# Moving the q and k transposes of a fused attention and gated-MLP kernel from TensorE to the DMA crossbar

## Chip, cores and metric

One core of one Trainium2 chip. The metric is the device time of one execution in microseconds (us); lower is better. Every quoted time is a median of several runs on one chip, unless it is said to be a single run. A verdict (faster, same, slower) compares a kernel with the kernel before by runs of the same rounds on the same chip, in the fast state only; some executions fall into a slower state, with a lower granted clock (the share of its full speed that the chip grants TensorE) and a time some per cent longer.

## The reference, cut to what matters

```python
# q, k, v: (8 batches, 8 heads, 576 tokens, 64); w_phi: (64, 128)
def phi(x):
    proj = einsum('bhsd,df->bhsf', x, w_phi)
    proj = proj - max(abs(proj), axis=-1)
    return concatenate([exp(proj), exp(-proj)], axis=-1)
q_p, k_p = phi(q), phi(k)
kv  = einsum('bhsf,bhsd->bhfd', k_p, v);  z = sum(k_p, axis=2)
num = einsum('bhsf,bhfd->bhsd', q_p, kv); den = einsum('bhsf,bhf->bhs', q_p, z) + 1e-6
x   = num / den                       # heads joined: (8, 576, 512)
h   = relu(x @ w_in);  u, v = halves(h)
out = (u * (w_spatial @ layernorm(v) + b_spatial)) @ w_out
```

Both projections of `phi` contract over the 64 features of a head, and both kernels feed TensorE q and k with features on the partitions (the 128 rows of on-chip memory). They arrive with tokens there. Something has to transpose them, and that is what the change is about.

## The kernel before

The work of the first half (attention features) is cut into 36 units: 32 "pairs" (two heads of one batch, 512 tokens) and 4 "shared tails" (the last 64 tokens of two batches, all heads). Unit 0 is the tail of the first two batches, units 1 to 4 are batch 0, 5 to 8 batch 1, 9 the next tail, 10 to 13 batch 2, and so on. The changed kernel swaps the first two: there unit 0 is the first pair of batch 0 and unit 1 the tail. The second half (gated MLP) is a queue of tasks, dealt out between the units at `RATE` tasks a unit.

```python
def load(b, parts=1):                                # landing tiles: two buffers each
    d = dict(q=ld.tile([P, H, NB * D], BF16, tag="q_bf"), k=ld.tile([P, H, NB * D], BF16, tag="k_bf"),
             v=ld.tile([P, H * NB, D], FP32, tag="v_f"))
    ...                                              # k and q by GpSimd (f32 to bf16 on the way)
    nc.sync.dma_start(out=d["v"]..., in_=main_ap(v, b))                  # v by SyncE

def a_transpose(u):                                  # one unit ahead of its use
    pt = psum.tile([P, 2, 4, P], BF16, tag="bank")
    for i, x in enumerate((src["k"], src["q"])):
        for j in range(4):
            nc.tensor.transpose(out=pt[:, i, j, :], in_=blk, identity=ident)     # L191
    nc.scalar.copy(out=u["kT"], in_=pt[:, 0])                                    # L194
    nc.vector.tensor_copy(out=u["qT"], in_=pt[:, 1])                             # L195

def a_keys(u):      # projection of k on TensorE, max on VectorE, exp on ScalarE
def a_scale(u):     # em = exp(-max) on ScalarE; vs = v * em on GpSimd (two multiplies, about 1.04 us each)
def a_kv(u):        # TensorE: kf^T vs, needs vs
...
for i in range(NU + 4):
    step(i)
    if i == 0:
        load(1); load_weights()                      # w_in, w_spatial, w_out by GpSimd
    elif u and u["pair"] and u["pj"] == 0 and 1 <= u["b"] < B - 1:
        b = u["b"] + 1
        load(b)                                      # one batch ahead
        if b % 2 == 0: load_tail(b // 2)
```

GpSimd therefore does two things in one order: it issues all k, q and weight loads, and it multiplies v. That order is not the order of this source text: when the kernel is built, a scheduler sorts the instructions of each engine.

Of the kernel before, what the change touches and what calls it, by code (L numbers as in the profile page):

```python
# [16 lines left out]
def kernel(  # L17
# [54 lines left out]
    def load_tail(g):  # L72
        d = dict(
            q=ld.tile([P, H, D], BF16, tag="q_tl", name="q_tl", bufs=2),
            k=ld.tile([P, H, D], BF16, tag="k_tl", name="k_tl", bufs=2),
            v=ld.tile([P, H, D], FP32, tag="v_tl", name="v_tl", bufs=2),
        )
        gs[g] = d
        for t, x in ((d["k"], k), (d["q"], q)):
            for i in range(2):  # L80
                nc.gpsimd.dma_start(out=t[i * TL:(i + 1) * TL], in_=tail_ap(x, 2 * g + i))
        for i in range(2):
            nc.sync.dma_start(out=d["v"][i * TL:(i + 1) * TL], in_=tail_ap(v, 2 * g + i))

    def load(b, parts=1):
        d = dict(
            q=ld.tile([P, H, NB * D], BF16, tag="q_bf", name="q_bf"),
            k=ld.tile([P, H, NB * D], BF16, tag="k_bf", name="k_bf"),
            v=ld.tile([P, H * NB, D], FP32, tag="v_f", name="v_f"),
        )  # L90
        st[b] = d
        n = H // parts
        for i in range(parts):
            nc.gpsimd.dma_start(out=d["k"][:, i * n:(i + 1) * n], in_=main_ap(k, b, i * n, n))
            nc.gpsimd.dma_start(out=d["q"][:, i * n:(i + 1) * n], in_=main_ap(q, b, i * n, n))
        nc.sync.dma_start(out=d["v"].rearrange("p (h c) d -> p h (c d)", h=H), in_=main_ap(v, b))
# [7 lines left out]
    make_identity(nc, ident)  # L104
    load_tail(0)
    load(0, parts=4)
# [75 lines left out]
    def a_transpose(u):  # L182
        src = st[u["b"]] if u["pair"] else gs[u["g"]]
        pt = psum.tile([P, 2, 4, P], BF16, tag="bank", name="pt")
        for i, x in enumerate((src["k"], src["q"])):
            for j in range(4):
                if u["pair"]:
                    blk = x[:, 2 * u["pj"] + j // 2, (j % 2) * P:(j % 2 + 1) * P]
                else:
                    blk = x[:, 2 * j:2 * j + 2, :]  # L190
                nc.tensor.transpose(out=pt[:, i, j, :], in_=blk, identity=ident)  # L191
        u["kT"] = a1.tile([P, 4, P], BF16, tag="kT", name="kT")
        u["qT"] = a1.tile([P, 4, P], BF16, tag="qT", name="qT", bufs=3)
        nc.scalar.copy(out=u["kT"], in_=pt[:, 0])  # L194
        nc.vector.tensor_copy(out=u["qT"], in_=pt[:, 1])  # L195
# [28 lines left out]
    def a_scale(u):  # L224
        em = small.tile([P, 2, H], FP32, tag="em", name="em")
        for s, sc in ((0, -1.0), (1, 1.0)):
            nc.scalar.activation(out=em[:, s, :], in_=u["mk"], func=AF.Exp, bias=0.0, scale=sc)  # L227
        if u["pair"]:
            pj = u["pj"]
            vs = feat.tile([P, 2, H, DS], BF16, tag="vs", name="vs", bufs=4)  # L230
            for s in range(2):
                nc.gpsimd.tensor_tensor(out=vs[:, s, :, 0:D], in0=st[u["b"]]["v"][:, pj * H:(pj + 1) * H, :],  # L232
                                        in1=em[:, s, :].unsqueeze(2).to_broadcast([P, H, D]), op=ALU.mult)
            nc.gpsimd.tensor_copy(out=vs[:, :, :, D:DA].rearrange("p i n o -> p i (n o)"), in_=em)
            u["vs"] = vs
        else:
            d = gs[u["g"]]
            vs = vst[u["g"] % 2]
            for bl in range(2):
                r = slice(bl * TL, (bl + 1) * TL)  # L240
                for s in range(2):
                    nc.gpsimd.tensor_tensor(out=vs[r, bl, s, :, 0:D], in0=d["v"][r],
                                            in1=em[r, s, :].unsqueeze(2).to_broadcast([TL, H, D]), op=ALU.mult)
                nc.gpsimd.tensor_copy(out=vs[r, bl, :, :, D:DA].rearrange("p i n o -> p i (n o)"), in_=em[r])
# [224 lines left out]
    for g in range(G):  # L469
        units.append(dict(pair=False, g=g, i=len(units)))  # L470
        for b in (2 * g, 2 * g + 1):
            for pj in range(NP):
                units.append(dict(pair=True, g=g, b=b, pj=pj, i=len(units)))
    NU = len(units)
# [29 lines left out]
    RATE = 4.0  # L504
# [8 lines left out]
    def step(i):  # L513
        n, u, w, z, y, x = (unit(i + d) for d in (1, 0, -1, -2, -3, -4))
        if i == 0:
            a_transpose(u)
        if u:
            a_keys(u)
            a_scale(u)
# [7 lines left out]
        if n:  # L527
# [76 lines left out]
```

## Time and profile before

| | before |
|---|---|
| time, median of 3 (range) | 343.94 us (343.77 to 346.18) |
| profiled span, granted clock | 346.0 us, 0.985 |
| busy TensorE / VectorE / ScalarE / GpSimd | 292.3 / 269.5 / 235.1 / 139.2 us |
| start of unit 1 / 9 / 19 / 35 | 20.8 / 70.5 / 151.4 / 284.7 us |

### The profile page before, as it was taken

The numbers are of one execution on the slowest core, as the hardware profiler recorded it, in microseconds if no ns is written. First come the engines' busy times: TensorE is split into PE (matmuls) and PEld (weight loads), VectorE is DVE, ScalarE is ACT, GpSimd is POOL, SyncE is SP. The second block draws the span as 40 slices with busy tenths as digits, with TensorE's granted clock in tenths as the row PEclk, the third lists the DMA queues.
The fourth block names the chain that finished last, engine by engine and source line by source line (L and its number), as shares of the span: only waits on it lengthen the run. The fifth ranks groups of instructions, "written<-read, shape, count | busy, mean of one in ns | idle before, by whom it ended". The sixth has DMA issues, their size and how long they took to land.

```text
span 346.0 us, 8470 instructions
## 1 busy us (share of the span) xinstructions
PE 292.3 (84%) x3370; PEld 196.6 (57%) x3370; DVE 269.5 (78%) x696; ACT 235.1 (68%) x514; POOL 139.2 (40%) x199
## 2 busy tenths in 40 slices
PE   0266888877899799998888999997986999999995
PEld 0155766545566567665655766765654766655441
DVE  5397999696795999979988997878788798375350
ACT  3089887757659687798867856985975845642723
POOL 8479936654243344264543342524234222001010
PEclk9998999998999999999999999999998999999999
DMA  7999994921029402930374019630000000520404
GB/s 179 221 184 196 194 206 56 140 81 31 2 24 237 122 2 25 240 118 2 34 92 121 3 10 156 247 109 2 3 1 2 2 0 16 200 63 0 140 0 136
DMA packets 45372, 31.13 MB, mean 90 GB/s; under 512 B 14546, under 2 KB 40210, under 8 KB 45332
## 3 DMA queue, kind: packets, MB, share of 16 engines
q0 software_dynamic: 27536, 11.71, 27.7%
q1 hardware_dynamic: 17796, 18.88, 17.9%
q8 instruction: 26, 0.43, 0.5%
q14 instruction: 14, 0.11, 0.1%
HBM read 32.85 MB, written 9.44 MB: 122 GB/s over the span
## 4 chain that ended last, share of the span: by engine, by line
DVE 41%; PE 35%; ACT 8%; POOL 7%; DMA 4%; issue 2%; POOLq 0%; SPq 0%; ACTq 0%
PE po L451 9%; DVE mk L212 7%; DVE mq L221 6%; DVE stats L362 4%; PE ps L428 4%; ACT kf L215 4%; PE pu L407 4%; DVE x L306 4%; PE ps L200 3%; DVE uT L431 3%; PE pq L270 3%; DMA q_tl<-in_q_dram 3%; DVE mhl L250 3%; DVE mhl L251 3%; DVE vn L387 2%; POOL rstd L369 2%
## 5 line engine op out<-in xcount | busy, mean ns | idle before, releaser
L232 POOL TENSOR_TENSOR vs<-v_f,em 128x512 bf16<-128x512 f32 x64 | 65.5, 1043 | 93.5 <-ACT em L227 88.2
L215 ACT ACTIVATE kf<-ps 128x512 bf16<-128x512 f32 x144 | 76.3, 623 | 25.5 <-DVE mk L212 24.9
L283 ACT ACTIVATE qf<-pq 128x512 bf16<-128x512 f32 x128 | 66.6, 622 | 26.7 <-PE pq L270 26.2
L212 DVE TENSOR_REDUCE mk<-ps 128x4 f32<-128x512 f32 x72 | 46.8, 676 | 2.2 <-PE ps L200 2.0
L221 DVE TENSOR_REDUCE mq<-ps 128x4 f32<-128x512 f32 x72 | 46.0, 676 | 0.0
L407 PE MATMUL pu<-xT,w_in_bf 128*128 128x512 bf16 x128 | 34.3, 393 | 3.8 <-DVE x L306 1.2
L453 ACT COPY ob<-po 128x512 f32<-128x512 f32 (+1 forms) x38 | 22.9, 606 | 20.8 <-issue 12.5
L266 PE MATMUL pq<-qT,wphi 128*128 128x256 bf16 x128 | 31.7, 274 | 4.3 <-DVE kv L300 2.1
L362 DVE BATCH_NORM_STATS2 stats<-vr 128x6 f32<-128x512 bf16 (+1 forms) x38 | 25.5, 676 | 12.2 <-ACT vr L361 12.0
L359 PE MATMUL pv<-w_in_bf,xT 128*128 128x512 bf16 x128 | 32.2, 379 | 3.0 <-DVE mq L221 1.7
L428 PE MATMUL ps<-w_spT,vn 128*128 128x512 bf16 x128 | 34.0, 380 | 0.7 <-DVE vn L387 0.7
L270 PE MATMUL pq<-mT,sel 128*128 128x128 bf16 x256 | 28.0, 222 | 5.5 <-DVE mT L256 5.5
L451 PE MATMUL po<-w_out_bf,uT 128*128 128x512 bf16 x128 | 31.8, 379 | 0.1
L194 ACT COPY kT<-pt 128x512 bf16<-128x512 bf16 x36 | 22.2, 617 | 13.9 <-PE pt L191 11.8
L200 PE MATMUL ps<-wphi,kT 128*128 128x256 bf16 x144 | 23.6, 280 | 7.0 <-ACT kT L194 3.2
L270 PEld LDWEIGHTS <-sel 128*128 128x128 bf16 x256 | 22.9, 99 | 11.5 <-issue 9.2
L361 ACT ACTIVATE vr<-pv 128x512 bf16<-128x512 f32 (+1 forms) x38 | 23.1, 624 | 8.6 <-PE pv L359 8.2
L296 PEld LDWEIGHTS <-kf 128*128 128x128 bf16 x512 | 23.8, 99 | 6.9 <-issue 1.3
L431 DVE TENSOR_TENSOR uT<-ps,uT 128x512 bf16<-128x512 f32 x32 | 21.8, 683 | 7.5 <-PE ps L429 7.5
L315 PEld LDWEIGHTS <-qf 128*128 128x128 bf16 x512 | 20.4, 97 | 11.0 <-issue 6.3
L409 ACT ACTIVATE uT<-pu 128x512 bf16<-128x512 f32 x32 | 19.6, 618 | 9.3 <-PE pu L407 9.1
L306 DVE TENSOR_TENSOR x<-pn,rc 128x256 bf16<-128x256 f32 x64 | 25.4, 416 | 0.5
(108 smaller groups left out, 606.4 us busy)
## 6 DMA issues: line engine op xcount, KB each, us to landing
v_f<-in_v_dram SPq DMA_DIRECT2D x8, 1024.0 KB, 8.5
out_dram<-ob SPq DMA_DIRECT2D x32, 256.0 KB, 2.5
k_bf<-in_k_dram POOLq DMA_DIRECT2D x7, 512.0 KB, 6.2
q_bf<-in_q_dram POOLq DMA_DIRECT2D x7, 512.0 KB, 7.9
v_tl<-in_v_dram SPq DMA_DIRECT2D x8, 128.0 KB, 4.5
w_in_bf<-in_moe_w_in_dram POOLq DMA_DIRECT2D x1, 1024.0 KB, 8.7
out_dram<-ob SPq DMA_DIRECT2D x8, 128.0 KB, 2.3
k_tl<-in_k_dram POOLq DMA_DIRECT2D x8, 64.0 KB, 8.0
```

The source lines that it names most:

```text
L200: nc.tensor.matmul(out=ps[:, 2 * x:2 * x + 2, :], lhsT=xT[:, 2 * half + x, :], rhs=wphi2, start=True, stop=True)
L212: nc.vector.tensor_reduce(out=u["mk"][:, hs], in_=pk, axis=AX.X, op=ALU.max, apply_absolute_value=True)
L215: nc.scalar.activation(out=u["kf"][:, s, hs, :], in_=pk, func=AF.Exp, bias=0.0, scale=sc)
L221: nc.vector.tensor_reduce(out=u["mq"][:, 4 * half:4 * half + 4], in_=pq, axis=AX.X, op=ALU.max, apply_absolute_value=True)
L232: nc.gpsimd.tensor_tensor(out=vs[:, s, :, 0:D], in0=st[u["b"]]["v"][:, pj * H:(pj + 1) * H, :], in1=em[:, s, :].unsqueeze(2).to_broadcast( ...
L270: nc.tensor.matmul(out=pq[:, 2 * par + x, :], lhsT=sel[:, j, :], rhs=m, start=False, stop=(x == 1))
L283: nc.scalar.activation(out=qf[:, s], in_=pq, func=AF.Exp, bias=0.0, scale=sc)
L306: nc.vector.tensor_tensor(out=x, in0=pn[r, :, 0:D], in1=rc[r].to_broadcast([n, 4, D]), op=ALU.mult)
L362: nc.vector.bn_stats(out=stats[r], in_=dst[r])
L407: nc.tensor.matmul(out=pu, lhsT=w_in_bf[:, kc, dc * P:(dc + 1) * P], rhs=d["xT"][:, kc, :], start=(kc == 0), stop=(kc == KC - 1))
L428: nc.tensor.matmul(out=ps, lhsT=d["vn"][:, sp, cs], rhs=w_spT[:, sp, 0:T0], start=(sp == 0), stop=False)
L451: nc.tensor.matmul(out=po[r], lhsT=lhs(dc), rhs=w_out_bf[:, dc, :], start=(dc == 0), stop=(dc == KC - 1))
```

## The change

Its intent: let the DMA crossbar do the transposes, so that TensorE loses 288 of them and ScalarE and VectorE lose 36 PSUM copies each. The diff, cut to its core:

```diff
+    def load_heads(b, h0, n):
+        for x, t in (("k", k), ("q", q)):
+            src = d[x][:, h0:h0 + n]
+            nc.gpsimd.dma_start(out=src, in_=main_ap(t, b, h0, n))
+            nc.sync.dma_start_transpose(out=d[x + "T"][:, 2 * h0:2 * (h0 + n), :],
+                                        in_=src.rearrange("p h x -> p (h x)"))
     (tile declarations)
-            q=ld.tile([P, H, NB * D], BF16, tag="q_bf", name="q_bf"),
-            k=ld.tile([P, H, NB * D], BF16, tag="k_bf", name="k_bf"),
+            q=ld.tile([P, H, NB * D], BF16, tag="q_bf", name="q_bf", bufs=1),
+            k=ld.tile([P, H, NB * D], BF16, tag="k_bf", name="k_bf", bufs=1),
+            kT=ld.tile([P, 2 * H, P], BF16, tag="kT", name="kT"),
+            qT=ld.tile([P, 2 * H, P], BF16, tag="qT", name="qT"),
     (tails: the same, k_tl, q_tl and v_tl from two buffers to one)
-    load_tail(0)
-    load(0, parts=4)
+    alloc(0); load_heads(0, 0, 4); load_tail(0); load_v(0); load_heads(0, 4, 4)
-    def a_transpose(u): ...                          # the 8 transposes and 2 copies
+    def a_transposed(u): ...                         # only picks slices of kT, qT
+        eng = nc.vector if u["i"] < 2 else nc.gpsimd # v scaling of the first two units
+    units[0], units[1] = units[1], units[0]          # batch 0 ahead of the first tail
-    RATE = 4.0
+    RATE = 4.1
```

More of the change, by code (lines that the diff above doesn't have):

```diff
@@ L73, in load_tail @@
         d = dict(
-            q=ld.tile([P, H, D], BF16, tag="q_tl", name="q_tl", bufs=2),
-            k=ld.tile([P, H, D], BF16, tag="k_tl", name="k_tl", bufs=2),
-            v=ld.tile([P, H, D], FP32, tag="v_tl", name="v_tl", bufs=2),
+            q=ld.tile([P, H, D], BF16, tag="q_tl", name="q_tl", bufs=1),
+            k=ld.tile([P, H, D], BF16, tag="k_tl", name="k_tl", bufs=1),
+            v=ld.tile([P, H, D], FP32, tag="v_tl", name="v_tl", bufs=1),
+            kT=ld.tile([P, NP, P], BF16, tag="kT_t", name="kT_t", bufs=2),
@@ L77, in load_tail @@
+            qT=ld.tile([P, NP, P], BF16, tag="qT_t", name="qT_t", bufs=2),
         )
         gs[g] = d
-        for t, x in ((d["k"], k), (d["q"], q)):
+        for t, x in (("k", k), ("q", q)):
             for i in range(2):
-                nc.gpsimd.dma_start(out=t[i * TL:(i + 1) * TL], in_=tail_ap(x, 2 * g + i))
+                nc.gpsimd.dma_start(out=d[t][i * TL:(i + 1) * TL], in_=tail_ap(x, 2 * g + i))
+            nc.sync.dma_start_transpose(out=d[t + "T"], in_=d[t].rearrange("p h d -> p (h d)"))
@@ L82, in load_tail @@
         for i in range(2):
             nc.sync.dma_start(out=d["v"][i * TL:(i + 1) * TL], in_=tail_ap(v, 2 * g + i))
-    def load(b, parts=1):
-        d = dict(
-            q=ld.tile([P, H, NB * D], BF16, tag="q_bf", name="q_bf"),
-            k=ld.tile([P, H, NB * D], BF16, tag="k_bf", name="k_bf"),
+    def load_heads(b, h0, n):
+        d = st[b]
+        for x, t in (("k", k), ("q", q)):
[3 more added lines that the diff above has]
+                                        in_=src.rearrange("p h x -> p (h x)"))
@@ L89, in load, with load_v, alloc @@
+    def load_v(b):
+        nc.sync.dma_start(out=st[b]["v"].rearrange("p (h c) d -> p h (c d)", h=H), in_=main_ap(v, b))
+    def alloc(b):
+        st[b] = dict(
+            q=ld.tile([P, H, NB * D], BF16, tag="q_bf", name="q_bf", bufs=1),
+            k=ld.tile([P, H, NB * D], BF16, tag="k_bf", name="k_bf", bufs=1),
+            kT=ld.tile([P, 2 * H, P], BF16, tag="kT", name="kT"),
+            qT=ld.tile([P, 2 * H, P], BF16, tag="qT", name="qT"),
             v=ld.tile([P, H * NB, D], FP32, tag="v_f", name="v_f"),
@@ L90, in load @@
         )
-        st[b] = d
-        n = H // parts
-        for i in range(parts):
-            nc.gpsimd.dma_start(out=d["k"][:, i * n:(i + 1) * n], in_=main_ap(k, b, i * n, n))
-            nc.gpsimd.dma_start(out=d["q"][:, i * n:(i + 1) * n], in_=main_ap(q, b, i * n, n))
-        nc.sync.dma_start(out=d["v"].rearrange("p (h c) d -> p h (c d)", h=H), in_=main_ap(v, b))
+    def load(b):
+        alloc(b)
+        load_heads(b, 0, H)
+        load_v(b)
     wphi2 = cpool.tile([P, 2 * F], BF16)
@@ L104 @@
     make_identity(nc, ident)
+    alloc(0)
+    load_heads(0, 0, 4)
     load_tail(0)
-    load(0, parts=4)
+    load_v(0)
+    load_heads(0, 4, 4)
     w_in_bf = cpool.tile([P, KC, DFF], BF16)
@@ L179, in transpose_spatial, with a_transposed @@
             nc.vector.tensor_copy(out=w_spT[row:row + 1, NB + bl, T0:S], in_=bsp_row[row:row + 1, T0:S])
-    def a_transpose(u):
-        src = st[u["b"]] if u["pair"] else gs[u["g"]]
-        pt = psum.tile([P, 2, 4, P], BF16, tag="bank", name="pt")
-        for i, x in enumerate((src["k"], src["q"])):
-            for j in range(4):
-                if u["pair"]:
-                    blk = x[:, 2 * u["pj"] + j // 2, (j % 2) * P:(j % 2 + 1) * P]
-                else:
-                    blk = x[:, 2 * j:2 * j + 2, :]
-                nc.tensor.transpose(out=pt[:, i, j, :], in_=blk, identity=ident)
-        u["kT"] = a1.tile([P, 4, P], BF16, tag="kT", name="kT")
-        u["qT"] = a1.tile([P, 4, P], BF16, tag="qT", name="qT", bufs=3)
-        nc.scalar.copy(out=u["kT"], in_=pt[:, 0])
-        nc.vector.tensor_copy(out=u["qT"], in_=pt[:, 1])
+    def a_transposed(u):
+        if u["pair"]:
+            js = slice(4 * u["pj"], 4 * u["pj"] + 4)
+            u["kT"], u["qT"] = st[u["b"]]["kT"][:, js, :], st[u["b"]]["qT"][:, js, :]
+        else:
+            u["kT"], u["qT"] = gs[u["g"]]["kT"], gs[u["g"]]["qT"]
     def by_token(xT, half):
@@ L231, in a_scale @@
             for s in range(2):
-                nc.gpsimd.tensor_tensor(out=vs[:, s, :, 0:D], in0=st[u["b"]]["v"][:, pj * H:(pj + 1) * H, :],
+                eng.tensor_tensor(out=vs[:, s, :, 0:D], in0=st[u["b"]]["v"][:, pj * H:(pj + 1) * H, :],
                                         in1=em[:, s, :].unsqueeze(2).to_broadcast([P, H, D]), op=ALU.mult)
-            nc.gpsimd.tensor_copy(out=vs[:, :, :, D:DA].rearrange("p i n o -> p i (n o)"), in_=em)
+            eng.tensor_copy(out=vs[:, :, :, D:DA].rearrange("p i n o -> p i (n o)"), in_=em)
             u["vs"] = vs
@@ L241, in a_scale @@
                 for s in range(2):
-                    nc.gpsimd.tensor_tensor(out=vs[r, bl, s, :, 0:D], in0=d["v"][r],
+                    eng.tensor_tensor(out=vs[r, bl, s, :, 0:D], in0=d["v"][r],
                                             in1=em[r, s, :].unsqueeze(2).to_broadcast([TL, H, D]), op=ALU.mult)
-                nc.gpsimd.tensor_copy(out=vs[r, bl, :, :, D:DA].rearrange("p i n o -> p i (n o)"), in_=em[r])
+                eng.tensor_copy(out=vs[r, bl, :, :, D:DA].rearrange("p i n o -> p i (n o)"), in_=em[r])
             d["vs"] = vs
@@ L473 @@
                 units.append(dict(pair=True, g=g, b=b, pj=pj, i=len(units)))
+    units[0], units[1] = units[1], units[0]
+    units[0]["i"], units[1]["i"] = 0, 1
     NU = len(units)
@@ L513, in step @@
     def step(i):
-        n, u, w, z, y, x = (unit(i + d) for d in (1, 0, -1, -2, -3, -4))
-        if i == 0:
-            a_transpose(u)
+        u, w, z, y, x = (unit(i - d) for d in range(5))
         if u:
+            a_transposed(u)
             a_keys(u)
@@ L526, in step @@
         fill(0.25)
-        if n:
-            a_transpose(n)
         if w:
```

## The prediction

> **What bounds the kernel now.** I read the shares by engine first, then the 40 slices, then the chain that ended last, then the groups that the change touches, then sums over one steady stretch.
>
> ```profile
> PE 292.3 (84%) x3370; PEld 196.6 (57%) x3370; DVE 269.5 (78%) x696; ACT 235.1 (68%) x514; POOL 139.2 (40%) x199
> ...
> PE   0266888877899799998888999997986999999995
> DVE  5397999696795999979988997878788798375350
> ...
> DMA  7999994921029402930374019630000000520404
> ```
>
> No engine is at its limit for the whole span. TensorE and VectorE trade the lead, ScalarE follows. TensorE has next to nothing in the first two slices (17 us), and at the right end (from about slice 33) it is near 9 while VectorE falls to 3 to 7. The DMA row is full for six slices and mostly idle afterwards.
>
> ```profile
> DVE 41%; PE 35%; ACT 8%; POOL 7%; DMA 4%; issue 2%; POOLq 0%; SPq 0%; ACTq 0%
> ```
>
> So the chain that sets the end hops between VectorE and TensorE, and the transfers have 4% of it. Followed in order of time, that is one transfer at the start and one of 4.86 us near 111 us:
>
> ```profile
> 4.97 9.84 DMA q_tl<-in_q_dram
> 14.81 0.14 issue
> 14.95 0.60 PE pt L191 x4
> 15.54 0.02 issue
> 15.56 0.59 ACT kT L194
> 16.16 0.05 issue
> 16.20 0.62 PE ps L200 x2
> ```
>
> The columns are start, length, what. The shared tail of the first two batches is loaded first, nothing real starts before its last piece has landed, and the first projection runs at 16.20 us.
>
> The groups that go (count, then busy us and mean ns, then idle before):
>
> ```profile
> L194 ACT COPY kT<-pt 128x512 bf16<-128x512 bf16 x36 | 22.2, 617 | 13.9 <-PE pt L191 11.8 <-PE pt L255 1.9
> L195 DVE COPY qT<-pt 128x512 bf16<-128x512 bf16 x36 | 14.9, 414 | 10.3 <-ACT kT L194 10.3
> L191 PE MATMUL pt<-ident,k_bf 128*128 128x128 bf16 x128 | 12.9, 225 | 0.2 <-DVE x L306 0.2
> L191 PE MATMUL pt<-ident,q_bf 128*128 128x128 bf16 x128 | 12.7, 222 | 0.0
> ```
>
> Third, a steady stretch from 100 us to the last unit's transposes, and the final part:
>
> ```profile
> 100.00:283.00 183.00, 165.95 (x1987) 114.39 (x1985) 156.46 (x403) 141.23 (x316) 72.03 (x99) 0.99 0.34 73
> 283.00:346.00 63.00, 57.85 (x530) 31.22 (x526) 33.91 (x90) 28.82 (x54) 6.36 (x11) 1.00 0.23 76
> ```
>
> The columns after the length are busy us of TensorE, its weight loads, VectorE, ScalarE, GpSimd, then the granted clock, DMA share and GB/s. In 183 us, TensorE is busy 91%, VectorE 85%, ScalarE 77%. The stretch holds 23 of the 36 units (23 copies of L195), so a unit takes 7.96 us. After 283 us only the second half of the kernel is left, 92% TensorE, and the change takes nothing from it.
>
> **What the Trainium skill says.** "VectorE: DVE Perf Modes", section "The three transpose paths", gives 390 ns for a 128x128 bf16 transpose on TensorE and 1309 ns through the DMA crossbar. The trace has 222 to 225 ns for one on TensorE, and eight in a row hold the chain for 0.45 us, so here they are pipelined and cheaper than the page's figure. The crossbar figure can't be checked in the kernel before, which has none. "DMA: Bandwidth & Descriptors", section "Latency and other measured facts", gives 261 GB/s for DMA transposes in one case and 350 to 400 when contiguous; its "Silent corruption: two transposing streams in flight at once" says that source rows of 256 bytes are what is moved. Its "Rules for kernel authors" asks a DMA that reads what an earlier one wrote to wait on that one's completion semaphore. The built kernel does so: each transpose on the SyncE queue waits for its GpSimd load. The page's two figures differ widely in what they mean here, and this is the main uncertainty.
>
> **The change part by part.**
>
> *Removed.* 288 transposes on TensorE (36 units x 8): 0.45 us a unit where they lie on the chain, 16.2 us in all; by busy time 13.49 us in the steady stretch, 0.59 us a unit. 36 copies on ScalarE, 22.2 us, 0.62 a unit. 36 copies on VectorE, 14.9 us, 0.41 a unit. One PSUM bank in a unit, which two engines had to empty. What of it lies on the chain now: I added its pieces over the whole span and got 19 pieces of L195 (6.3 us), ten groups of L191 (4.65 us) and five of L194 (2.6 us), 13.6 us. The rest ran beside other work.
>
> *What it is worth in the steady part.* Two ways. If a unit shrinks by what leaves VectorE, 0.41 us; if TensorE's 91% stays and its work falls from 165.95 to 152.46 us, the stretch takes 152.46/0.907 = 168 us, 15 us less, or 0.65 a unit. The chain sum is (13.6 - 1.2 for the first unit)/35 = 0.35 a unit, but that keeps every other wait: the pieces "copy of kT, then projection" in which one engine waits for another go altogether, and 13.9 and 10.3 us of idle time stand before those copies. I take 0.5 us for 33 units: 16.5 us.
>
> *Added.* 26 crossbar transposes on the SyncE queue, of 288 blocks of 128x128: 4 of 8 blocks, 14 of 16, 8 of 4. A full one reads and writes 512 KB. From the skill's 261 GB/s it would move in 2 us, plus some fixed time. From this trace: a queue's packet took 27.7% x 346 us x 16 / 27536 = 56 ns of one engine on average, and 2048 rows of 256 bytes over 16 engines come to 7.1 us. I estimate 5 to 8 us. A batch has two of them in some 35 us, and the loads run a batch ahead, so in the steady part they should be hidden. The order on the queues shows the price: the k and q buffers are now single, so GpSimd's load of the next batch waits for a transpose, and on SyncE a transpose that waits for TensorE to leave the old kT stands ahead of output stores and v loads. Both queues are in order. VectorE also takes the v scaling of the first two units: 6 multiplies, about 0.7 us each by L431 (683 ns for 128x512 from f32), 4 us, at a time when VectorE is not full.
>
> *Moved.* The first unit is now half of batch 0's heads, loaded first, with the 1 MB v loads behind its transpose in the SyncE order. In the trace before, a first load issued at 1.3 us beside those v loads made TensorE start at 11.67 us. Without them I put its landing at 7 us, the transpose done at 12, the first projection 4 us earlier than 16.20. GpSimd's part of the chain from 23.7 to 30.15 us (six weight loads' issue and the scaling) goes as well. But the transposes of q and of the tails come on SyncE after 2 MB of v and may land at 20 us or later, so of this I count 4 us. RATE 4.1 for 4.0 moves about 40 x 0.1 = 4 tasks of the second half, of roughly 1 us each, from the end into the steady part, which is nearly even: 0.
>
> *Sum.* 346.0 - 16.5 - 4 = 325.5 us of profiled span. The span is 1.006 of the timed median (346.0/343.94), so 323.6; I say 324.
>
> **The rivals.**
>
> 1. *The transfers become the bound.* With 1309 ns for each block one after another, 288 blocks take 377 us, and the kernel would take some 380 us. With my 7.1 us estimate, 18 full transposes' worth (288/16) take 128 us of all 16 engines, and the queues already take 46%, 160 us: 288 us of 325, 89%. That fits only if the work is spread evenly. For it: the DMA row is already full for the first 40 us. Against: from slice 11 on it is mostly idle, and SBUF to SBUF needs no HBM. Where it half fails, GpSimd and SyncE wait in order, scaling and outputs come late, and the time is about 340.
>
> 2. *VectorE keeps the bound.* It leads the chain (41%), and loses only 0.41 us in 7.96, and gets 4 us of scaling. Then 33 x 0.35 = 12 us and no gain at the start: 346 - 12 = 334, timed 332. For it: the long runs of VectorE pieces between 155 and 190 us. Against: VectorE waits 10.3 us at those very copies.
>
> 3. *All three engines benefit together.* TensorE, VectorE and ScalarE each lose 5 to 10% of their work and a whole round trip through PSUM; 0.75 us a unit and 6 us at the start would give 346 - 25 - 6 = 315, timed 313.
>
> 4. *A slow start.* If a transposed half batch takes 10 us and all six first ones run in a row on one queue, unit 3 waits until 40 us, and the start loses 8 us: 332.
>
> **Range and chances.** Rivals 2 to 4 lie between 313 and 332; a little outside for rival 1's mild form. Range 312 to 336. 2% faster means below 337.1. Only a real transfer bound, or a slow start together with rival 2, ends above it. Faster 0.84, within 2% 0.10, slower 0.06.
>
> **What would show it right or wrong.** Right: no ACT copy to kT and no DVE copy to qT; ScalarE busy near 213 us, VectorE near 259, TensorE near 264; a unit in the middle takes about 7.4 us; a full transpose lands 5 to 8 us after issue; the first projection at about 12 us; the last part as before, some 63 us long. Wrong: waits of TensorE for a transpose in the middle of the span, a DMA row of 8 or 9 throughout, GpSimd's v scaling held behind load issues for many us, or ScalarE's output copies waiting for stores that stand behind transposes. A first projection later than 16 us refutes the start. If the time falls by less than 7 us though the three busy sums fall as said, then the removed work was not on the path.

## More of the kernel before

The start of a unit is the start of its first max over the keys on VectorE. The prediction shows the page's lines. Two more views matter for what came. The first is the issue of w_in in the page's last part (kB written, median us from issue to landing); the second is GpSimd's timeline (start, length, line, what, and idle time before with what ended it):

```profile
w_in_bf<-in_moe_w_in_dram POOLq DMA_DIRECT2D x1, 1024.0 KB, 8.7
```

```profile
55.41 0.94 POOL L94 DMA_DIRECT2D k_bf<-in_k_dram  x1 [1.68 <-PE pt L255]
56.60 0.90 POOL L95 DMA_DIRECT2D q_bf<-in_q_dram  x1 [0.26 <-issue]
57.63 2.04 POOL L232 TENSOR_TENSOR vs<-v_f,em 128x512 bf16<-128x512 f32 x2
```

A load is issued, GpSimd waits next to nothing for its buffer, and the next scaling of v starts right behind it. That is how the two jobs of GpSimd live together here.

## The result, and the profile after

367.54 us, median of 4 (365.03 to 368.86), against 345.06 us for the kernel before in the same rounds: **slower**, ratio 1.064, 95% interval 1.056 to 1.072. A ratio in this text is the mean time of one kernel's fast runs over that of the other's of the same rounds, so it is not quite the ratio of the medians quoted. The profiled span is 366.9 us.

From the page of the changed kernel, with the shares by engine, the 40 slices and the chain:

```profile
PE 280.4 (76%) x3041; PEld 184.8 (50%) x3082; DVE 255.6 (70%) x669; ACT 216.4 (59%) x478; POOL 130.5 (36%) x186
...
PE   0105657549479997899776879999879699999995
DVE  3227965644377969996587788985898989567361
...
DMA  9998999999748078747940376369000000340303
...
PE 35%; DVE 23%; DMA 15%; POOL 9%; ACT 7%; SPq 5%; issue 5%; POOLq 0%; ACTq 0%; DVEq 0%
```

The work fell as intended (VectorE 269.5 to 255.6 us, ScalarE 235.1 to 216.4), but TensorE stands at 4 to 7 tenths in slices 3 to 11 (one 9 aside), that is up to about 110 us, where before it had 6 to 9. The DMA row is at 8 or 9 for the first ten slices, where before it fell off after the sixth. The chain got 15% of DMA, 9% of GpSimd and 5% of SyncE's sequencer. A TensorE sum near 264 us did not come, and could not: the records of the transposes overlap those of their neighbours, and without them the kernel before has a busy time of 280.0 us (counted over its trace), which is what came (280.4).

Two groups and two lists of issues:

```profile
L210 PE MATMUL ps<-wphi,kT 128*128 128x256 bf16 x128 | 21.5, 286 | 19.7 <-DMA kT<-k_bf 16.1
...
L92 POOL DMA_DIRECT2D k_bf<-in_k_dram x9 | 8.3, 922 | 52.4 <-DMA kT<-k_bf 46.0
```

```profile
w_in_bf<-in_moe_w_in_dram POOLq DMA_DIRECT2D x1, 1024.0 KB, 15.1
...
kT<-k_bf SPq DMA_TRANSPOSE x9, 4.7
```

From issue to landing a transpose of k takes 4.7 us (median of those whose landing the trace shows, half and full ones), even a little less than predicted; later than 120 us a full one takes 4.3 to 5.1 us, in the first 100 us up to 11.6 us, and one of q 19.3. But TensorE waits 16 us for them ahead of the projection of k, and GpSimd stands 46 us ahead of its loads of k, because the one landing buffer still waits for its transpose.

**Where in time it is lost.** The starts of the units, in us:

| unit | before | after | difference |
|---|---|---|---|
| 0 | 16.9 | 15.5 | -1.4 |
| 1 | 20.8 | 32.6 | +11.8 |
| 5 | 42.1 | 52.4 | +10.3 |
| 8 | 60.7 | 78.1 | +17.4 |
| 9 | 70.5 | 98.2 | +27.7 |
| 19 | 151.4 | 174.4 | +23.0 |
| 20 | 159.7 | 189.2 | +29.5 |
| 35 | 284.7 | 307.2 | +22.5 |

(Units 0 and 1 are swapped by the change, so these two rows compare places in the order and not the same work.) Three losses (unit 1, units 5 to 9, unit 20), and between them a steady gain: 4.7 us over ten units from 9 to 19, about 0.5 us a unit.

The first loss, in SyncE's timeline of the changed kernel:

```profile
6.95 1.33 SPq L93 DMA_TRANSPOSE kT<-k_bf  x1
8.33 0.65 SPq L97 DMA_DIRECT2D v_f<-in_v_dram  x1
...
10.97 0.40 SPq L97 DMA_DIRECT2D v_f<-in_v_dram  x1
11.42 14.85 SPq L93 DMA_TRANSPOSE qT<-q_bf  x1
```

The k of the first half batch is transposed early. The q, whose load had landed at 9.16 us, goes behind two v loads of 1 MB. Merely issuing its transpose holds SyncE for 14.85 us, and it lands at 30.7 us. The profile puts this time down to the load of w_spatial as the releaser; but that load landed at 28.07 us, after SyncE had gone on at 26.27, and the one semaphore that this instruction waits for had all its counts from the q load at 9.16. So I read it as time to issue. The next four transposes stand behind it, the tail's among them, for which unit 1 waits.

The second loss, in the chain that ended last (start, length, what):

```profile
65.31 6.20 DMA kT_t<-k_tl
...
72.67 1.42 POOL k_tl L83 x2
74.09 6.08 issue
80.19 0.74 POOL q_bf L92
80.92 11.56 DMA kT<-k_bf
...
93.02 0.94 POOL k_bf L92
93.98 2.05 POOL vs L243 x2
```

From 65 us on nothing on this chain computes until the last line. GpSimd issues a load, waits until the buffer of the next load has been transposed, issues that, waits again. The scaling at 93.98 us, on which TensorE's next matmuls wait, stands behind these loads in GpSimd's order. And they were not urgent: the loads of the tails of units 18 and 27 are all issued by 85 us, and the k of batches 3 and 4, first used in units 14 and 19, at 66.33 and 93.02 us, ahead of the scalings of units 5 and 8.

The transposes that GpSimd waits for were themselves waiting, on SyncE, for TensorE to leave the tile that they write: those issued at 66.61 and 80.92 us until 72.2 and 86.4 us. SyncE's longest waits of this kind (total us, times, longest us), first in the changed kernel, then in e8, an experiment below, with e8's waits for the loads of k:

```profile
SPq L93 <- PE ps L210: 86.1, 8, 24.3
```

```profile
SPq L94 <- DMA k_bf<-in_k_dram: 69.9, 8, 14.7
...
SPq L94 <- PE ps L211: 7.6, 3, 4.8
```

So the waits are chained over three engines: GpSimd's load waits for a transpose, the transpose on SyncE for TensorE, and TensorE for the scaling that stands behind the load. What these waits of SyncE cost by themselves was not measured.

So after reading I had two theories that the trace alone could not part. **A, order:** GpSimd stands at early loads whose buffers are held by transposes, and the scaling behind them stops TensorE. **B, volume:** the transposes and loads of the first 100 us are too much, everything lands late, and any order would suffer. SyncE's queue, where stores and v loads stand with the transposes, was a third suspect for the start and for unit 20.

### The profile page after: what moved, and what is told of

Its sections match the earlier page's. It is cut to its first block, busy times and chain, and to the rows that moved or that the text cites. A ratio compares the mean times of both kernels' runs of the same rounds, so it can differ in the third digit from the quotient of the medians.

```text
span 366.9 us, 7879 instructions
## 1 busy us (share of the span) xinstructions
PE 280.4 (76%) x3041; PEld 184.8 (50%) x3082; DVE 255.6 (70%) x669; ACT 216.4 (59%) x478; POOL 130.5 (36%) x186
## 4 chain that ended last, share of the span: by engine, by line
PE 35%; DVE 23%; DMA 15%; POOL 9%; ACT 7%; SPq 5%; issue 5%; POOLq 0%; ACTq 0%; DVEq 0%
PE po L462 8%; PE ps L439 7%; DMA wsp<-in_moe_w_spatial_dram 5%; DVE stats L373 4%; DMA kT<-k_bf 4%; ACT kf L225 3%; SPq L93 3%; PE ps L210 3%; DVE mk L222 3%; DVE mq L231 3%; DVE vn L398 3%; DMA kT_t<-k_tl 3%; PE pu L418 2%; POOL rstd L380 2%; DMA out_dram<-ob 2%
## 5 line engine op out<-in xcount | busy, mean ns | idle before, releaser
L225 ACT ACTIVATE kf<-ps 128x512 bf16<-128x512 f32 x144 | 76.1, 622 | 56.7 <-DVE mk L222 56.5
L243 POOL TENSOR_TENSOR vs<-v_f,em 128x512 bf16<-128x512 f32 x62 | 63.6, 1048 | 75.6 <-ACT em L237 72.4
L222 DVE TENSOR_REDUCE mk<-ps 128x4 f32<-128x512 f32 x72 | 47.0, 678 | 13.0 <-PE ps L210 12.8
L373 DVE BATCH_NORM_STATS2 stats<-vr 128x6 f32<-128x512 bf16 (+1 forms) x38 | 25.6, 679 | 17.7 <-ACT vr L372 17.5
L418 PE MATMUL pu<-xT,w_in_bf 128*128 128x512 bf16 x116 | 31.8, 387 | 7.5 <-DVE x L317 4.6
L277 PE MATMUL pq<-qT,wphi 128*128 128x256 bf16 x128 | 33.1, 288 | 5.0 <-ACT kf L225 3.0
L210 PE MATMUL ps<-wphi,kT 128*128 128x256 bf16 x128 | 21.5, 286 | 19.7 <-DMA kT<-k_bf 16.1
L464 ACT COPY ob<-po 128x512 f32<-128x512 f32 (+1 forms) x38 | 22.3, 614 | 24.1 <-issue 12.3
L307 PE MATMUL pv<-vs,kf 128*128 128x65 bf16 x512 | 26.0, 199 | 13.6 <-POOL vs L245 13.6
L307 PEld LDWEIGHTS <-kf 128*128 128x128 bf16 x512 | 24.7, 101 | 19.6 <-issue 14.0
L210 PE MATMUL ps<-wphi,qT 128*128 128x256 bf16 x128 | 21.7, 291 | 16.8 <-DMA qT<-q_bf 14.9
L370 PE MATMUL pv<-w_in_bf,xT 128*128 128x512 bf16 x121 | 32.7, 395 | 0.8 <-ACT vr L372 0.3
L326 PEld LDWEIGHTS <-qf 128*128 128x128 bf16 x512 | 21.5, 100 | 11.8 <-issue 6.9
L372 ACT ACTIVATE vr<-pv 128x512 bf16<-128x512 f32 (+1 forms) x38 | 22.0, 625 | 8.9 <-PE pv L370 8.1
L92 POOL DMA_DIRECT2D k_bf<-in_k_dram x9 | 8.3, 922 | 52.4 <-DMA kT<-k_bf 46.0
## 6 DMA issues: line engine op xcount, KB each, us to landing
w_in_bf<-in_moe_w_in_dram POOLq DMA_DIRECT2D x1, 1024.0 KB, 15.1
```

Of the source, the lines that this page charges most:

```text
L210: nc.tensor.matmul(out=ps[:, 2 * x:2 * x + 2, :], lhsT=xT[:, 2 * half + x, :], rhs=wphi2, start=True, stop=True)
L222: nc.vector.tensor_reduce(out=u["mk"][:, hs], in_=pk, axis=AX.X, op=ALU.max, apply_absolute_value=True)
L225: nc.scalar.activation(out=u["kf"][:, s, hs, :], in_=pk, func=AF.Exp, bias=0.0, scale=sc)
L243: eng.tensor_tensor(out=vs[:, s, :, 0:D], in0=st[u["b"]]["v"][:, pj * H:(pj + 1) * H, :], in1=em[:, s, :].unsqueeze(2).to_broadcast([P, H, ...
L307: nc.tensor.matmul(out=pv[:, hh, s, :], lhsT=u["kf"][:, s, 4 * hh + c, :], rhs=u["vs"][:, s, 4 * hh + c, 0:DA], start=(c == 0), stop=False)
L373: nc.vector.bn_stats(out=stats[r], in_=dst[r])
```

## The experiments

Twelve kernels ran, each beside the kernel before on the same chip. Unless said otherwise the edit is against the changed kernel and the result is correct.

### e1: no transposes at all (wrong result)

```diff
-            src = d[x][:, h0:h0 + n]
+            src = d[x + "T"].rearrange("p (h y) x -> p h (y x)", h=H)[:, h0:h0 + n]
             nc.gpsimd.dma_start(out=src, in_=main_ap(t, b, h0, n))
-            nc.sync.dma_start_transpose(...)
```

> Wrong result on purpose: k and q are loaded straight into the tiles that the crossbar transposes filled, so neither TensorE nor the crossbar transposes anything; all else is the changed kernel. Theory (the removed engine work is worth about 0.5 us a unit, and the loss of 28 us in the first nine units plus 7 us near the 20th is made by the transposes on the SyncE queue and the waits of GpSimd for them): the span falls from 367 us to some 320 to 328, with the second unit starting before 25 us and the ninth before 60. Rival (the engines were not helped by the removal, or the lowered clock or the new order of units is what costs): 345 or more.

Measured: 331.32 us (330.93 to 332.62), ratio 0.960; the span of 328.9 us is just above the 320 to 328 that the theory expected. Against the changed kernel, 36.2 us is the whole price of the crossbar transposes (367.54 - 331.32). What they save has the size that was predicted, and the price is the step that went wrong. 33 of the 36 us are there by unit 9 (98.2 against 65.2 us).

### e4: the change's order without its transposes

```diff
+    (a_transpose with TensorE and both copies as before; two landing buffers; no crossbar)
```

The new order of units, the VectorE scaling of the first two and `RATE` stay.

> The kernel before, with the transposes still on TensorE, but with the change's order: first half batch ahead of the tails, first pair unit before the tail unit, scaling of the first two units on VectorE, rate 4.1. Theory (the order itself is harmless and gains a little): 338 to 345 us, second unit before 21 us. Rival (the new order causes the late start): 350 us or more.

Measured: 348.47 us (345.89 to 348.67), ratio 1.007 (0.999 to 1.015). Neither expectation had this time. The new order of the first loads gains nothing. The 4 us that I had booked for it don't exist even without the crossbar: unit 1 starts at 20.8 us as before. From e4 to e1, which ran in the same rounds, it is 17.2 us. Of this e1 has 2.3 us already at unit 1 (18.5 against 20.8); between the starts of units 1 and 35 the two traces differ by 15.2 us, 0.45 us a unit.

### e2: half-batch landing tiles, two of each

```diff
-            src = d[x][:, h0:h0 + n]
+            src = ld.tile([P, 4, NB * D], BF16, tag=x + "_bf", name=x + "_bf")
```

Each batch is loaded and transposed in halves.

> The k and q landing tiles hold half a batch each and there are two of each, in the same SBUF; loads and transposes go by half batches (52 instead of 26 less the tails'). Theory that GpSimd's load issues wait for the one buffer and hold the v scaling back: GpSimd's waits for transposes before k and q loads (63 us in the changed kernel) fall to under 30 us, units 5 to 9 lose less than 8 us instead of 18, the time is some 350 to 358 us. Rival (the transfers themselves are too slow there, or SyncE's order is what delays): no gain, 363 to 375 us, with more issue time on SyncE. The first wait, before the second unit, should stay near 15 us in both.

Measured: 362.47 us (361.74 to 364.19), ratio 1.048; a miss. GpSimd still waits 53.6 us for transposes, and unit 9 starts at 95.9 us. More and smaller buffers did not end the waiting; why not was still open here. The start missed its expectation too: unit 1 starts at 25.8 us instead of 32.6. In this build w_in goes out at 25.13 us instead of 8.71, and the first q transpose holds SyncE for 7.28 us instead of 14.85 (see e10).

### e3: the first v loads from ScalarE

```diff
-        nc.sync.dma_start(out=st[b]["v"]..., in_=main_ap(v, b))
+        eng = nc.scalar if b < 2 else nc.sync
+        eng.dma_start(out=st[b]["v"]..., in_=main_ap(v, b))
```

> The v loads of batches 0 and 1 are issued by ScalarE, so the first transposes don't stand behind 2 MB of v on SyncE's queue; they run beside it instead. Theory (the transpose of q is held at its issue because the queue is full of v): its issue takes 2 to 6 us instead of 14.85, the second unit's keys start at 20 to 25 us instead of 32.6, and the time falls by 7 to 12 us to some 356 to 360 us. Rival (the 16 engines' total work in the first 30 us is the limit, whichever queue holds it): the second unit stays at 29 us or later and the time within 3 us of 367.

Measured: 364.88 us (363.69 to 366.23), ratio 1.056. The v loads now went out even before k. The q transpose was issued at 14.65 us, held SyncE 1.64 us only, and still landed at 32.55 us; unit 1 started at 34.4 us. So at the start the place on SyncE is not the cause by itself. With the v loads on another queue the transpose came just as late.

### e7: the output stores from ScalarE

```diff
-        nc.sync.dma_start(out=dst, in_=ob)
+        nc.scalar.dma_start(out=dst, in_=ob)
```

> The changed kernel with the output stores issued by ScalarE, so they don't queue behind a v load and a transpose on SyncE. Theory (the 6.5 us lost at the 20th unit are ob buffers held by stores that landed 8 us after issue behind 1 MB of v): the jump goes, the time falls by 3 to 7 us to 360 to 364 us; stores land about 2.5 us after issue. Rival (the DMA engines are shared, whichever queue issues, or ScalarE loses more by issuing 40 stores): 366 us or more.

Measured: 370.88 us (370.37 to 374.31), ratio 1.071; a miss. The step at unit 20 fell from 14.8 to 9.6 us, but the step to unit 21 grew from 5.5 to 12.8 us at another wait: a scaling on GpSimd behind a transposed q that took 11 us to land.

### e5: transposes that no one waits for (wrong result)

```diff
+            idle = ld.tile([P, 2 * H, P], BF16, tag="idle_" + x, name="idle_" + x, bufs=1)
-            nc.sync.dma_start_transpose(out=d[x + "T"][...], in_=...)
+            nc.sync.dma_start_transpose(out=idle[...], in_=...)        # on top of e1
```

> Wrong result on purpose: as e1_no_transpose, k and q are loaded straight into the tiles that the projections read, but SyncE also issues all the transposes of the changed kernel, from those tiles into scratch tiles that no engine reads. The DMA engines and SyncE's queue have the same work, the projections and GpSimd's loads don't wait for it (only v loads and stores stand behind it). Theory A (it is the waiting that costs, of the projections for transposes and of GpSimd's queue for the single buffers): 331 to 342 us, ninth pair near 70 us. Theory B (the 16 engines' extra traffic in the first 100 us delays all loads, so the wait is for volume): 355 to 367 us, with the unit that starts the second group at 90 us or later.

Measured: 349.92 us (347.67 to 350.95), ratio 1.008, between the ranges of the two theories. At the time I read this as a tie: the transposes' traffic costs 18.6 us over e1, and waiting for them another 17.6 us. That reading did not last. In e5 SyncE stands 102 us (64.3 + 38.0) for the k and q loads that its transposes read, with v loads and stores behind it, and stores land up to 9.0 us after issue; so it measures an order along with the traffic. e8, which has all transposes and uses them, comes out 5 us faster than e5. But e5 does tell about the second loss, where its unit 9 starts at 75.1 us instead of 98.2. Between 60 and 100 us, the changed kernel, e5 and e8 in this order (the last figure is GB/s):

```profile
60.00:100.00 40.00, 25.70 (x289) 18.82 (x288) 21.18 (x63) 17.50 (x40) 18.04 (x26) 0.80 1.23 152
```

```profile
60.00:100.00 40.00, 31.17 (x343) 21.19 (x346) 31.70 (x83) 26.24 (x60) 20.27 (x28) 0.91 1.11 185
```

```profile
60.00:100.00 40.00, 31.48 (x365) 21.35 (x365) 33.22 (x90) 27.03 (x63) 20.01 (x29) 0.96 0.72 111
```

e5 moves more in this stretch than the changed kernel, with DMA engines nearly as busy (the column before, 1.11 and 1.23), and gets through it without the loss.

### e6: TensorE transposes for the first two batches and their tail, crossbar for the rest

```diff
+    FIRST = 1
-            nc.sync.dma_start_transpose(...)
+            if b // 2 >= FIRST:
+                nc.sync.dma_start_transpose(...)    # else a_transpose(u) on TensorE, as before
```

With the half-batch tiles of e2.

> Batches 0 and 1 and their tail are transposed on TensorE as in the kernel before, batches 2 to 7 by the crossbar (half-batch landing tiles as in e2_halves, the changed order else). Theory (all but some 5 us of the loss lies in the first nine units, where the loads fill the DMA engines anyway; later a unit gains 0.5 us): the start is as in e4_order_only, 26 units gain up to 13 us, some 5 to 7 us go at the stores near the 20th unit: 335 to 344 us, below the kernel before. Rival (the transposes cost wherever they are): 350 us or more.

Measured: 360.57 us (359.48 to 362.15), ratio 1.038; a miss, and the most telling one. Up to unit 8 the kernel is in time (64.9 us), then unit 9 starts at 91.0 us. The loss left the start and moved to where the crossbar sets in. Between 61 and 85 us its chain alternates between a transpose of k (3.34 us from 61.27, 3.30 from 70.35, 5.80 from 78.73) and a load of k (4.47 from 65.86, 4.39 from 74.21), and then comes a GpSimd scaling at 86.80 us. A loaded start can't be the whole cause.

### e8: loads behind the scalings that they don't have to precede

One order edge on GpSimd, no wait, no other transfer:

```diff
+            scaled[u["i"]] = eng.tensor_copy(out=vs[:, :, :, D:DA]..., in_=em)      # end of a pair's scaling
...
             b = u["b"] + 1
-            load(b)
-            if b % 2 == 0: load_tail(b // 2)
+            with tc.issue_after(scaled[i].ins):      # order on GpSimd only
+                load(b)
+                if b % 2 == 0: load_tail(b // 2)
```

> The changed kernel with one thing held: on GpSimd the k and q loads of batch b+1 (b at least 1) and of the tail that goes with it stand behind the v scaling of batch b's first unit in program order, instead of where the scheduler put them (there the tail loads of the third and fourth pair of batches and the loads of batches 2 to 4 stand ahead of the scalings of units 2 to 12). No transfer is added or removed. Theory A (GpSimd stands at loads whose landing buffer waits for a transpose, and the scaling behind them holds TensorE): GpSimd's wait of 63 us for transposes nearly goes, unit 9 starts at 72 to 85 us instead of 98, and the time is 345 to 353. Theory B (the transposes come late because the first 100 us have too many transfers): the loads come later still, unit 9 stays above 92, and the time is 362 or more. The start (unit 1 at 32.6 us) should not move under either.

Measured: 345.04 us (343.47 to 347.79), ratio 0.995 (0.988 to 1.002); unit 9 at 78.8 us. Both inside what theory A expected; GpSimd's waits fell from 63.2 to 23.5 us. By itself this does not rule out theory B, since the edge also puts transfers off (111 GB/s between 60 and 100 us instead of 152); e5 with its 185 GB/s speaks against volume alone, for this stretch. The edge also lets the scheduler sort SyncE's queue anew, and the runs don't part what GpSimd's order and what SyncE's is worth. GpSimd's timeline where the changed kernel lost its 20 us:

```profile
54.77 2.05 POOL L244 TENSOR_TENSOR vs<-v_f,em 128x512 bf16<-128x512 f32 x2 [1.96 <-ACT em L238]
...
56.89 0.95 POOL L93 DMA_DIRECT2D k_bf<-in_k_dram  x1
57.83 0.90 POOL L93 DMA_DIRECT2D q_bf<-in_q_dram  x1
...
61.43 2.10 POOL L244 TENSOR_TENSOR vs<-v_f,em 128x512 bf16<-128x512 f32 x2
```

The loads go out without idle time before them, as in the kernel before. And GpSimd's waits for a landing buffer (total us, times, longest us), the changed kernel first and then e8:

```profile
POOL k_bf L92 <- DMA kT<-k_bf: 46.0, 5, 23.4
...
POOL q_bf L92 <- DMA qT<-q_bf: 17.2, 4, 6.1
```

```profile
POOL k_bf L93 <- DMA kT<-k_bf: 23.5, 1, 23.5
```

The only wait that stays is the one of the second batch in the first 33 us. Output stores land within 4.4 us of their issue in all of e8, up to 8.1 us in the changed kernel, and the step at unit 20 is 10.6 us, where e1, without any transpose, has 10.4 and e4 10.7 (8.3 before). So what the crossbar added to the third loss went with the order as well.

What is left against e1 is 13.7 us (345.04 - 331.32), and unit 1 is 14.2 us later than in e1 (32.7 against 18.5). At unit 9 it is 13.6 us, at unit 28 15.8 us and at unit 35 17.0 us. So after the start all transposes together, and all their traffic, cost some 3 us in these two traces (the medians are of different rounds and too coarse to tell): there they are nearly hidden.

### e9: the order of e8 on e6

> The same order of loads on top of e6 (TensorE transposes for the first two batches and their tail, crossbar for the rest, half-batch landing buffers). Theory A: the start stays as in e6 (unit 1 at 19 us, unit 8 at 65), the 26 us lost between units 8 and 9 shrink to 8 to 12, and 24 of 33 units keep their 0.5 us: 335 to 345, close to or below the kernel before. Theory B: unit 9 stays at 85 us or more and the time at 356 or more.

Measured: 336.38 us (335.69 to 336.76), ratio 0.969 (0.964 to 0.975): faster than both kernels. Unit 8 starts at 56.7 us, unit 9 at 67.5. From e6 to e9 the one order edge takes off 24.2 us, 0.069 of the ratio (1.038 to 0.969), as much as from the changed kernel to e8 (1.064 to 0.995).

### e10: the weights later

```diff
         if i == 0:
             load(1)
-            load_weights()
+        elif i == 2:
+            with tc.issue_after(scaled[i].ins):
+                load_weights()                      # on top of e8
```

> e8, and the five weight loads (w_in, the three parts of w_spatial, w_out) stand behind the scaling of unit 2 on GpSimd instead of in the first 10 us, so the first 30 us have 2 to 3 MB less to read. If the volume in the first 30 us is what holds the first transposes (q of the first half batch lands at 30.7 us), that transpose lands at 20 to 24 us, unit 1 starts at 22 to 27 instead of 32.6, and the time is 4 to 8 us below e8. If it is the order on SyncE (two 1 MB v loads ahead of the transpose), unit 1 stays above 29 and the time within 3 us of e8. If the weights then come late for the second half, TensorE waits for w_spatial or w_in, and part of it is lost again.

Measured: 348.95 us, but two of its four runs were slow ones (clock about 0.95); the fast two took 346.48 and 341.58 us, and the time is unclear. Its profile fell in the slow state too, so I use from it only what the start shows. There the q transpose holds SyncE for half as long, lands at 22.5 us, and unit 1 starts at 24.4 us instead of 32.7:

```profile
11.32 7.23 SPq L94 DMA_TRANSPOSE qT<-q_bf  x1
```

So fewer bytes in the first 30 us bring the start forward; here no load of w_spatial is in flight either, which the profile had named as what held this transpose. The order on SyncE has its part in it: in the changed kernel, e2, e8, e10 and e12 the q transpose lands 0.85 to 0.96 us after the second v load that was issued ahead of it (29.75 and 30.70 us in the changed kernel, 21.56 and 22.46 in e10). In e3, without v on this queue, it lands at 32.55, just before w_spatial. The time itself missed its 4 to 8 us below e8, since the order was wrong at another place: TensorE waits 15.8 us for w_spatial, which its program needs in unit 4, and unit 5 starts at 60.6 us.

### e12: only w_in and w_out later

```diff
+    def load_w_in_out(): ...                        # the two lines taken out of load_weights()
+        elif i == 2:
+            with tc.issue_after(scaled[i].ins):
+                load_w_in_out()                     # on top of e8
```

> e8 with w_in and w_out alone behind the scaling of unit 2; the three parts of w_spatial, for which TensorE waited 16 us in e10, stay in the first 10 us. w_in is 2 MB of float32. If the volume in the first 30 us sets the start, the first q transpose lands at 24 to 27 us instead of 30.7, unit 1 starts at 26 to 29 instead of 32.7, nothing waits for w_spatial, and the time is 3 to 6 us below e8 (338 to 342). If the loss at the start is of another kind, it stays within 1.5 us of e8.

Measured: 340.26 us median of six, one of them slow (350.24); the five fast ones 337.09 to 340.97, with a median of 339.69. Ratio 0.978 (0.973 to 0.984), which straddles the 2% line, so the verdict is unclear: probably faster than the kernel before. Unit 1 starts at 28.2 us:

```profile
11.39 10.80 SPq L94 DMA_TRANSPOSE qT<-q_bf  x1
```

With less weight volume the same issue took 14.83 us (e8), 10.80 (e12), 7.23 (e10). The changed kernel put the weights into that place unasked: before, w_in was issued at 24.2 us, behind the scaling of the tail on GpSimd; here it goes out at 8.71 us and takes 15.1 instead of 8.7 us to land. Moving that scaling to VectorE explains part of this: e4, which has the move but no crossbar, issues w_in at 15.50 us. There the loads of batch 1 (9.73 and 13.33 us) still stand in front; in the changed kernel they wait for the single landing buffers and come behind. An early w_in does no harm where the start needs no crossbar: e6 issues it at 9.35 us and has unit 1 at 19.3.

### e11: control, the order of e8 on the kernel before

```diff
+            with tc.issue_after(scaled[i].ins):      # on top of the kernel before
+                load(b) ...
```

> Control: the kernel before (TensorE transposes, two landing buffers) with the same rule as e8, loads of batch b+1 behind the scaling of batch b's first unit on GpSimd. Theory A says that in the kernel before a landing buffer comes free only when TensorE has transposed it, so the scheduler could not pull loads far ahead (its GpSimd order already has only one batch and two tails ahead), and nothing is to be had: ratio 0.99 to 1.01, 341 to 349 us. If the order alone is worth several per cent there too, what e9 gains over the kernel before is not the crossbar's: ratio 0.98 or less.

Measured: 345.22 us (344.56 to 346.98), ratio 0.996 (0.992 to 1.000): the same. The order has something to repair only with the crossbar, and what e9 gains over the kernel before does not come from the order alone.

## Why the prediction was wrong, and where it was right

By the steps of its sum, "346.0 - 16.5 - 4 = 325.5":

1. **"I take 0.5 us for 33 units: 16.5 us": right in size, with some luck.** e4 to e1 gives 0.45 us a unit, and the changed kernel gains 0.47 between units 9 and 19. The highest of its three ways (0.65 by TensorE) rests on a wrong difference: the transposes' 13.49 us overlap with other matmuls, and the trace without their records has 159.6 us of TensorE in that stretch and not 152.46. That gives 159.6/0.907 = 176 us, 0.31 a unit. So all three ways were too low (0.31, 0.35, 0.41), and the compromise was saved by one that was over-counted.

2. **"in the steady part they should be hidden": the step that failed.** The estimate under it was near: 4.7 us to land against the 5 to 8 predicted, and in e8 the transposes cost some 3 us after the start. (Its packets took 26 ns each and not 56; and a further block of 32 KB took about 0.16 us, some 205 GB/s, less than the 261 that the prediction quotes.) But "hidden" asks for more than a short transfer. It asks that nothing else stand in line behind it. I had seen both parts, single buffers and in-order queues, and listed "GpSimd's v scaling held behind load issues for many us" as a sign of being wrong, but priced it at 16 us in a rival (340 against 324) and gave it little chance. e8 shows the price: 22.5 us (367.54 - 345.04) of the 36.2. The mechanism: in the kernel before, with two landing buffers, a load waits until TensorE has transposed the batch two before it. With the crossbar it waits for the transpose of the batch just before it, which in turn waits until TensorE has left the kT or qT of the batch three before it. So loads may run one batch further ahead, and the built order has loads that are needed tens of us later ahead of scalings that are needed now; GpSimd stands at each of them, and through this chain of waits TensorE stands too. That the scheduler did this because it takes DMAs for quick is my guess; that the order did the damage is shown, by e8 and again by e9 against e6.

3. **"of this I count 4 us": wrong in sign.** Unit 0 did start earlier, but by 1.4 us (15.5 against 16.9), because the first transpose landed at 14.77 us and not at 12 (its load had landed at 6.94, as predicted at 7); and unit 1 came 11.8 us later. e4 shows that the order of the loads is worth nothing by itself. One reading under the step was wrong: TensorE's start at 11.67 us did not wait for the load issued at 1.3 us, which landed at 5.75, but for the second piece of that k, issued at 3.58 and landed at 11.54. e10 and e12 show that the q transpose waits for the volume around it: moving weights out brings unit 1 back by 8.3 and 4.5 us. Rival 4 ("a slow start", 8 us lost) was the right one, still too small: its "six first ones run in a row on one queue" is what SyncE's timeline shows, but the cost was in the loads ahead of them, not in six times 10 us. What I missed is that the weight loads would move ahead by 15 us, once their predecessor on GpSimd went to VectorE and batch 1's loads had to wait for the single buffers.

The terms from the medians: +2.2 us from before to e4 (348.47 - 346.28, within 2%, so "the same"), -17.2 from e4 to e1, +13.7 from e1 to e8 (the start), +22.5 from e8 to the changed kernel (the order edge). The sum is +21.2; measured in its own rounds, +22.5 (367.54 - 345.06). These medians are of different rounds and chips; by the ratios to the kernel before, times 346 us, the terms are +2.4, -16.4, +12.3 and +23.8, so each is good to some 2 us.

4. **The rivals.** Rival 1 named the right engines and was of the right kind in its mild form ("GpSimd and SyncE wait in order, scaling and outputs come late, about 340") but too mild; and it asked for the transfers to be the bound, which e5 and e8 speak against after the start. Rivals 2 and 3 speak of the gain, not of the loss. The last part stayed as predicted: 59.7 us from the start of unit 35 to the end (366.9 - 307.2), before 61.3 (346.0 - 284.7).

What stays open: whether the lower granted clock (0.80 between 60 and 100 us in the changed kernel, 0.96 in e8) is only a consequence of TensorE's idle time or cost something of its own was not tried. How much of the 14 us at the start is volume and how much the order on SyncE is shown only in part: e12 takes back 4.5 us at unit 1, e10 8.3 us, and e5, where no projection waits for the transposes, starts unit 1 at 25.6 us, 7.1 us after e1. For the second loss, the shares of GpSimd's and SyncE's order are open.

## What to carry to other kernels

When a producer moves from a compute engine to a DMA, it changes what holds the loads back. Here they could run one batch further ahead, and the built order put them in front of urgent work. Before crediting a transfer as hidden, list what stands behind it on each in-order engine, and ask for each piece of urgent work which less urgent issue could stand in front of it. If a loss appears, try an order edge before more buffers: here one edge was worth 22.5 us, while smaller tiles with two buffers (e2) brought 5.

## What the Trainium skill lacked or had wrong

- "VectorE: DVE Perf Modes", section "The three transpose paths", gives 1309 ns for a 128x128 transpose through the crossbar and 390 ns on TensorE. In these runs one DMA of 4 blocks landed 2.4 us after issue at best, one of 8 blocks 3.1 us and one of 16 blocks 4.3 us: about 0.16 us for each further block ((4.3 - 2.4)/12), on some 1.8 us of fixed time. TensorE's took 222 to 225 ns each, and overlapped: eight in a row held the chain for 0.45 us. The table does not say that its figure can't be multiplied by the blocks.
- "DMA: Bandwidth & Descriptors", section "Issuing engines are not separate DMA queues", says that the time on the sequencer to start a DMA "is usually small relative to the DMA itself". For a transpose behind 1 MB loads it was not, if I read its time on SyncE rightly: 1.3 us when quiet, 7.2 to 14.9 us in the first 30 us of e10, e12, e8 and the changed kernel. What the section says of shared engines agrees with e3: with the v loads on another engine the transpose landed no earlier (32.55 against 30.7 us).
- The same page's "Rules for kernel authors" advises to issue a DMA early and to wait for it late. The rule itself does not add that a load issued early whose buffer is still held stops its issuing engine, with all compute behind it: 63.2 us of such waits on GpSimd in the changed kernel (46.0 + 17.2) against 23.5 in e8, and 22.5 us of the time.
- No page that I read gives the crossbar's cost beside other work: 36,864 packets of 256 bytes at 26 ns each on average, about 60 us of 16 engines in sum, cost some 3 us after the start (e8 against e1, by their traces).
